# Chunked attention and a top-1 mixture of experts: the opening expert chosen a batch earlier, and the outputs' transposes ahead of the next attention product

## The chip, the cores and the metric

One core of a Trainium2 chip. The metric is the time of one execution on the device, in microseconds (us); the median of several runs is given. Engines are called by their names or by the short ones of the profile: PE is TensorE's matmuls, PEld its weight loads, DVE VectorE, ACT ScalarE, POOL GpSimd, SP SyncE, which issues most transfers.

## The reference

```python
# attention: 4 batches, 8 heads, 768 tokens, head size 64; chunks of 32 queries
for c in range(nc):
    k_full = concat([mem_k, k[l_start:r_end]])    # 8 memory keys, 16 left, 32 own, 8 right
    scores = scale * q_c @ k_full.T
    a = exp(scores - max); a /= a.sum() + 1e-9
    out[chunk] = a @ v_full
x = out.transpose(0, 2, 1, 3).reshape(3072, 512)
# mixture of experts: 8 experts, 512 -> 1024 -> 512, one expert for each token
logits = x @ w_gate + modality_bias[modality_id]
e_idx = argmax(logits); gate = softmax(logits)[e_idx]
for e in range(8):
    out[mask] = gate[mask] * (relu(x[mask] @ w1[e]) @ w2[e])
```

All is float32. The expert of a token is known only when all its heads are done.

## The kernel before, in words

**Attention.** 16 units of two heads, each in two halves (hf) of 384 tokens, make 32 iterations i. In iteration i TensorE is given, in this order: `scores` of i (L351), `exps_t` of i-1 (L369, transposes of the scores less their maximum; ScalarE then writes their exponentials, PT), the transposes of the next unit's keys (`trans_k`, hf=0, copied by ScalarE into kbd, four copies) or queries (`trans_q`, hf=1, two copies to qT), `attend` of i-1 (L381, which reads PT and v, tile vw), and `trans_x` of i-2 (L404), which transposes the normalized outputs xb for the router; ScalarE copies them to xT. VectorE takes maximum and difference (mx, sb) of i, and den, reciprocal and xb of i-1 (`normalize`). Only in iterations 29 and 30 does trans_x stand ahead of attend. The rows of xb are written to DRAM, xd, once for each unit (POOL issues).

**Routing.** When a batch's four units are done, `route(b)` is appended to a list, and `pump` issues its pieces in between: logits (L541), transposes of them, argmax on VectorE, ranks of the tokens by matmul (L581 to L586), one-hot tiles l and a (L654, L656, two of six pairs on POOL, four on VectorE), and matmuls (L664) that put token numbers into `table`. The last batches are issued faster than others (KB = 3 for batch 2).

**Start of the experts.** Slots of 256 tokens with one expert each follow. Weights are split into a high and a low part, three products for each of the two layers, with ScalarE casting and VectorE or POOL subtracting. Which expert slot 0 takes is chosen in route(2), from the counts of three batches; its place (regs0) is read by SP, which then issues the eight w1 transfers of 256 KB (`load_w(0, 0)`), and by POOL, which gathers the rows (`gather(0)`, indirect transfers). At the end of iteration 29 a loop `while routing` issues all that is left of routing ahead of these two; route(3) follows among the first mm1, the matmuls of the first layer.

**Order.** TensorE, SP and POOL run in the order in which the code is written. ScalarE and VectorE do so until iteration 26 (MAN), and from there to the second slot a scheduler orders them.

Of the kernel before, what the change touches and what calls it, by code (L numbers as in the profile page):

```python
# [9 lines left out]
F32 = mybir.dt.float32  # L10
F32R = mybir.dt.float32r
BF16 = mybir.dt.bfloat16
I32 = mybir.dt.int32
# [7 lines left out]
P = 128  # L21
# [8 lines left out]
EMPTY = 4096.0  # L30
MAGIC = 12582912.0
NTAIL = 8
NEXTRA = 7
HEAD = 3
LAST = 3
ROW_R1 = HEAD + NTAIL + 1
# [5 lines left out]
NACT = 2  # L42
CPOOL = (10, 12, 13, 14, 15)
MAN = 26
KB = 3
NSPIN = 11
NR = 32
# [6 lines left out]
def tile_chunk_attention_top1_moe(  # L54
# [129 lines left out]
    listed, turn0, ends, tail_no, at_r1, at_x = (rows[:, i:i + 1] for i in range(6))  # L184
    quarter, edge = [const.tile([P, 1], F32, name=f"quarter{i}") for i in range(2)]
    noth = const.tile([64, E], F32, name="noth")
    col0 = const.tile([64, E], F32, name="col0")
    nsl = const.tile([1, 2], I32, name="nsl")
    regs0 = const.tile([1, 2], I32, name="regs0")
# [224 lines left out]
    def pump(k, pe=False):  # L414
        k *= KB if routing and routing[0][2] == B - 2 else 1
        while k > 0 and routing:
            g, wait, b, since = routing[0]
            if wait:
                if not pe or now[0] < since + (wait == "late" or b < B - 2) + (wait == "late" and b < B - 2):
                    return  # L420
                pe = False
            r = next(g, None)
            if r is None:
                routing.pop(0)
                return
            routing[0] = (g, r if r != "v" else "", b, now[0])
            k -= r == "v"
# [14 lines left out]
    def plan_early():  # L442
        vec = nc.vector
        full = rounded("full", 1.0 / 256, 127.0 / 256 - 0.498)
        free, score, top, one, three, row = (
            plan_new("free"), plan_new("score"), plan_new("top", 1), plan_new("one"), plan_new("three", 3, E), plan_new("row", 3))
        vec.tensor_sub(free, full, ohg[0:64])
        vec.scalar_tensor_tensor(score, free, 0.0, prio, op0=ALU.is_gt, op1=ALU.mult)
        vec.reduce_max(top, score, axis=AX.X)
        vec.tensor_scalar(one, score, top, None, op0=ALU.is_equal)  # L450
        vec.tensor_tensor(three, base, one.unsqueeze(1).to_broadcast([64, 3, E]), op=ALU.mult)
        vec.reduce_sum(row, three, axis=AX.X)
        vec.tensor_copy(regs1, row)

    def plan_rest():
# [1 line left out]
        vec = nc.vector  # L457
        full, free, used = plan["full"], plan["free"], plan["one"]
        vec.tensor_sub(free, free, used)
        vec.tensor_add(used, used, ohg[0:64])  # L460
        tail = rounded("tail", 1.0 / 256, 0.498)
        vec.tensor_sub(tail, tail, full)
        small, score, top, first = plan_new("small"), plan["score"], plan["top"], plan_new("first")
# [72 lines left out]
    def route(b):  # L536
# [77 lines left out]
        yield "v"  # L614
        nc.vector.tensor_add(ac, ac, hi)
        yield "v"
        if b == B - 2:

            cm = sm.tile([P, 1], F32, name="cm")
            cb = sm.tile([P, E], F32, name="cb")  # L620
            nc.vector.tensor_copy(cb, rk[:, NT, :])
            yield "v"
            nc.vector.reduce_max(cm, cb, axis=AX.X)
            yield "v"
            nc.vector.tensor_scalar(cb, cb, cm, None, op0=ALU.is_equal)
            yield "v"
            nc.vector.tensor_mul(cb, cb, rev[:, 0])
            yield "v"
            nc.vector.reduce_max(cm, cb, axis=AX.X)
            yield "v"  # L630
            nc.vector.tensor_scalar(regs0[:, 0:1], cm[0:1], -1.0, float(E), op0=ALU.mult, op1=ALU.add)
            yield "v"
            nc.vector.tensor_scalar(regs0[:, 1:2], cm[0:1], -float(HI), float(E * HI), op0=ALU.mult, op1=ALU.add)
            yield "v"
# [29 lines left out]
            nc.tensor.matmul(tb[:, 0:192], l1, a1, start=(t == 0), stop=(t == NT - 1))  # L664
        nc.vector.tensor_sub(table if b < B - 1 else tab_i[:, 0:192], table, tb[:, 0:192])
        yield "v"
        if b == B - 2:
            nc.vector.tensor_scalar(ohg, rev[:, 0], cm, None, op0=ALU.is_equal)
            yield "v"
            nc.vector.tensor_scalar(noth, rev[0:64, 0], cm[0:64], None, op0=ALU.not_equal)  # L670
            yield "v"
            nc.vector.scalar_tensor_tensor(prio, ohg[0:64], 16.0, rev[0:64, 0], op0=ALU.mult, op1=ALU.add)
            yield "v"
            nc.vector.tensor_copy(base[:, 0], iota[0:64, 0:E])
            yield "v"
            nc.vector.tensor_copy(base[:, 1], noth)
            yield "v"
            nc.vector.scalar_tensor_tensor(base[:, 2], ohg[0:64], 2.0, col0, op0=ALU.mult, op1=ALU.add)
            yield "v"
        if b < B - 1:  # L680
            ts = sm.tile([P, E], F32, name="ts")
# [48 lines left out]
    def keep(opening):  # L730
        if not opening:
            nc.gpsimd.tensor_copy(ix_out, ix_now)  # L732
            nc.gpsimd.tensor_copy(gate_out, gate_now)  # L733
        nc.gpsimd.tensor_copy(ix_now, ix)  # L734
        for t in range(2):
            nc.gpsimd.tensor_copy(gate_now[:, t:t + 1], xg[t][:, DM:DM + 1])  # L736

    def gather(row):
        src, reg = (table, regs0[0:1, 1:2]) if row == 0 else (tab_i, (regs1 if row < 2 else regs)[row:row + 1, 2:3])
        rows = N - S if row == 0 else N  # L740
        col = nc.values_load(reg, engines=[mybir.EngineType.Pool], min_val=0, max_val=E * HI - 2,
                             skip_runtime_bounds_check_because="clamped to the table on chip")
        nc.gpsimd.tensor_copy(ix, src[:, ds(col, 2)])
        nc.gpsimd.tensor_scalar(gx, ix, float(rows - 1), None, op0=ALU.min)  # L744
        for t in range(2):
            nc.gpsimd.indirect_dma_start(  # L746
                out=xg[t], out_offset=None, in_=xd[0:rows],
                in_offset=bass.IndirectOffsetOnAxis(ap=gx[:, t:t + 1], axis=0))

    def gather_rest(i):  # L750
        row = (ROW_R1 - 1, ROW_R1)[i]
# [146 lines left out]
    for i in range(n + 2):  # L898
        live = i < n
        u, hf = units[i] if live else (NU, i % 2)  # L900
        now[0] = i
        if i == MAN:
            man.close()
        if live and i < n - 1:
            scores(u, hf)
        if 1 <= i <= n:
            exps_t(*units[i - 1])
        if live:
            less_max(u, hf)
            pump(1)  # L910
        if u + 1 < NU and hf == 0:
            trans_k(u + 1)
            regroup_q(u + 1)
            pump(3)
            store_k(u + 1, 1, 0, nc.scalar.copy)
            store_k(u + 1, 0, 0, nc.scalar.copy)
            store_k(u + 1, 0, 1, nc.scalar.copy)
            store_k(u + 1, 1, 1, nc.scalar.copy)
            pump(3)
        elif u + 1 < NU:  # L920
            share_v(u + 1)
            if u + 2 < NU:
                mem_keys(u + 2, nc.gpsimd)
            trans_q(u + 1)
            store_q(u + 1, 0)
            store_q(u + 1, 1)
            pump(5)
        elif live:
            pump(5)
        first = i in (n - 3, n - 2)  # L930
        if first:
            trans_x(*units[i - 2])
        if i == n - 2:
            scores(*units[i + 1])
        if 1 <= i <= n:
            attend(*units[i - 1])
        if i == n:
            trans_x(*units[i - 2])
            trans(0)
            trans(1)  # L940
            conv(4)
            conv(5, nc.gpsimd)
            normalize(*units[i - 1])
            mm1(0)
        if i > n:
            mm1(1)
        if i >= 2 and not first and i != n:
            trans_x(*units[i - 2])
        if 1 <= i < n:
            normalize(*units[i - 1])  # L950
            pump(1)
        if i >= 2:
            u2, hf2 = units[i - 2]
            if hf2 == 1 and u2 % 4 == 3:
                routing.append((route(u2 // 4), True, u2 // 4, 0))
        if i == 1:
            routing.append((more_constants(), False, -1, 0))
        if i == 6:
            assert not routing
            bias_rows()  # L960
        if i < n:
            pump(1, True)
        if live and hf == 0:
            if 0 < u < NU - 3:
                load_qk(u + 3)
            if u >= 1 and u - 1 + NVW < NU:
                load_v(u - 1 + NVW)
        if (u, hf) == (NU - 2, 1):
            while routing:
                pump(99, True)  # L970
            c_ld.close()
            xp = ctx.enter_context(tc.tile_pool(name="xp", bufs=1, side="right"))
            ix = xp.tile([P, 2], I32, name="ix")
            gx = xp.tile([P, 2], I32, name="gx")
            xg = [xp.tile([P, XW], F32, name=f"xg{t}", align_bytes=256) for t in range(2)]
            xth, xtl = [xp.tile([P, 4, 256 + NR], F32R, name=f"xt{i}") for i in range(2)]
            hh, hl = [xp.tile([P, 8, 256], F32R, name=f"h{i}") for i in range(2)]
            load_w(0, 0)
            gather(0)
        elif u == NU - 1:  # L980
            conv(2 * hf)
            conv(2 * hf + 1, nc.gpsimd)
# [170 lines left out]
```

## Time and profile before

| | us |
|---|---|
| median of 3 runs | 443.09 (442.23 to 444.68) |
| profiled execution | 444.34 |
| its span | 442.5 |
| PE busy | 419.0 |
| DVE, ACT, POOL busy | 306.6, 269.4, 205.7 |

The span is the time from the first to the last instruction recorded. A busy PE includes pipelined matmuls whose ends are modelled. In a timeline a row's bracket is the idle time ahead of it and what ended it; in lists of waits the engine that waits, its line, the instruction waited for, the sum, the number and the longest are shown. The granted clock is given as a share of the full 2.4 GHz.

### The profile page before, as it was taken

What the parts mean: (1) busy time and instruction counts of PE and PEld (TensorE: products, weight loads), DVE (VectorE), ACT (ScalarE), POOL (GpSimd) and SP (SyncE); (2) the same over time, 40 slices, a digit from 0 to 9 for tenths busy, and PEclk for the clock granted to TensorE, in tenths of its full rate; (3) what the DMA queues carried; (4) which work ended last, traced back from release to release, by engine and by line L of the source; (5) the groups of instructions that cost most, each with busy time, mean ns of one, the idle gap of its engine ahead of it and who ended that gap; (6) DMA issues with size and microseconds to landing.
All of it is one profiled execution on the core that took longest, in us unless ns stands there. A gap on an engine that the chain in (4) does not pass through costs nothing. (4 is left out here: it accounts for less than half of the span.)

```text
span 442.5 us, 11878 instructions
## 1 busy us (share of the span) xinstructions
PE 419.0 (95%) x4053; PEld 355.7 (80%) x4053; DVE 306.6 (69%) x752; ACT 269.4 (61%) x537; POOL 205.7 (46%) x409
## 2 busy tenths in 40 slices
PE   7889999999986998999999999999999999999993
PEld 4667777777765886989888898989898988898982
DVE  7878597687796799657646366686868584959530
ACT  5857878778655763556456455666656665757521
POOL 7999769779677932651053305505031115220101
PEclk9989999999998999999999999999999999999998
DMA  7789878787465501277185977505596404340101
GB/s 203 206 234 252 243 189 256 210 236 210 122 179 175 193 4 52 96 208 233 53 259 164 246 206 243 180 13 170 127 240 229 139 5 147 99 143 1 48 1 47
DMA packets 78307, 69.31 MB, mean 157 GB/s; under 512 B 36763, under 2 KB 64563, under 8 KB 78228
## 3 DMA queue, kind: packets, MB, share of 16 engines
q1 hardware_dynamic: 71488, 48.84, 39.6%
q0 software_dynamic: 5888, 19.41, 14.2%
q8 instruction: 37, 0.61, 0.6%
q14 instruction: 42, 0.34, 0.3%
q10 hardware_dynamic: 852, 0.11, 0.2%
HBM read 81.25 MB, written 16.58 MB: 221 GB/s over the span
## 5 line engine op out<-in xcount | busy, mean ns | idle before, releaser
L803 PEld LDWEIGHTS tr<-xt,w 128*128 128x128 f32 x1152 | 140.9, 188 | 4.9 <-issue 2.7
L803 PE MATMUL tr<-xt,w 128*128 128x256 f32 (+1 forms) x1152 | 142.9, 284 | 1.9 <-PEq L1114 0.7
L813 PE MATMUL av<-wh,h 128*128 128x512 f32 x384 | 124.9, 397 | 0.0
L807 DVE SCALAR_TENSOR_TENSOR h<-tr,h 128x256 fp32r<-128x256 f32 x96 | 40.5, 422 | 66.1 <-ACT h L804 33.7
L813 PEld LDWEIGHTS av<-wh,h 128*128 128x128 f32 x384 | 72.1, 188 | 16.6 <-issue 0.4
L813 PE MATMUL av<-wl,h 128*128 128x512 f32 x192 | 75.5, 393 | 0.0
L804 ACT ACTIVATE h<-tr 128x256 fp32r<-128x256 f32 x96 | 36.7, 384 | 54.1 <-PE tr L803 42.4
L728 DVE TENSOR_TENSOR wl<-raw,wh 128x512 fp32r<-128x512 f32 x91 | 63.0, 693 | 7.2 <-ACT wh L726 0.4
L838 POOL DMA_INDIRECT out_dram<-o,ix x24 | 24.6, 1027 | 92.6 <-ACT o L834 89.5
L728 DVE TENSOR_TENSOR w<-raw,w 128x512 fp32r<-128x512 f32 x93 | 60.2, 686 | 5.3 <-ACT w L726 2.8
L301 POOL COPY vw<-vw 24x384 f32<-24x384 f32 (+1 forms) x128 | 60.1, 506 | 3.0 <-DMA vw<-in_v_dram 1.2
L726 ACT CAST wh<-raw 128x512 fp32r<-128x512 f32 x96 | 59.0, 615 | 0.4 <-DMA raw<-in_moe_w_dram 0.4
L726 ACT CAST w<-raw 128x512 fp32r<-128x512 f32 x96 | 52.9, 622 | 0.0
L343 ACT COPY kbd<-tr 64x672 f32<-64x672 f32 x62 | 48.3, 779 | 5.3 <-PE tr L337 4.2
L813 PEld LDWEIGHTS av<-wl,h 128*128 128x128 f32 x192 | 36.1, 188 | 7.7
L834 ACT ACTIVATE o<-av,gate 128x512 f32<-128x512 f32 x24 | 16.2, 688 | 39.1 <-PE av L813 30.6
L381 PE MATMUL av<-vw,PT 128*32 128x130 f32 x768 | 29.8, 286 | 7.5 <-ACT PT L371 6.2
L746 POOL DMA_INDIRECT xg<-xd,gx x24 | 27.1, 1127 | 16.9 <-POOL gx L744 5.7
L381 PEld LDWEIGHTS av<-vw,PT 128*32 128x32 f32 x768 | 20.4, 112 | 11.9 <-ACT PT L371 9.9
L351 PE MATMUL sc<-kbd,qT 128*32 128x128 f32 x768 | 28.2, 281 | 1.3 <-DVE kbd L343 1.3
L371 ACT ACTIVATE PT<-tr 128x384 f32<-128x384 f32 x32 | 15.8, 493 | 20.1 <-PE tr L369 16.8
L359 DVE TENSOR_REDUCE mx<-sc 128x6 f32<-128x384 f32 x32 | 18.4, 574 | 9.7 <-PE sc L351 9.5
(250 smaller groups left out, 518.4 us busy)
## 6 DMA issues: line engine op xcount, KB each, us to landing
raw<-in_moe_w_dram SPq DMA_DIRECT2D x192, 256.0 KB
k<-in_k_dram SPq DMA_DIRECT2D x16, 384.0 KB
q<-in_q_dram SPq DMA_DIRECT2D x16, 384.0 KB
xd<-xb POOLq DMA_DIRECT2D x16, 384.0 KB
vw<-in_v_dram SPq DMA_DIRECT2D x32, 184.0 KB
xs<-xg SPq DMA_DIRECT2D x14, 256.0 KB
xq<-xs SPq DMA_DIRECT2D x28, 128.0 KB
vw<-in_mem_v_dram SPq DMA_DIRECT2D x32, 48.0 KB
```

The source lines that it names most:

```text
L301: nc.gpsimd.tensor_copy(vw[r0:r0 + 24, c + 1:c + 1 + w, d], vw[r0 + 32:r0 + 56, c:c + w, d])
L343: copy(dst.rearrange("p c (i j) -> p c i j", j=2)[:, :, :, j], win)
L351: nc.tensor.matmul(sc[32 * j:32 * j + 32, t * P:(t + 1) * P], qT[:, 32 * c:32 * c + 32], kbd[:, c].rearrange("p h m -> p (h m)"), start=Tr ...
L381: nc.tensor.matmul(avb[32 * j:32 * j + 32, t * W:(t + 1) * W], PT[:, t * P + 32 * j:t * P + 32 * j + 32], vw[:, c, 0:W], start=True, stop= ...
L726: nc.scalar.copy(wh[i], raw[i])
L728: (eng or nc.vector).tensor_sub(wl[i][:, s], raw[i][:, s], wh[i][:, s].bitcast(F32))
L746: nc.gpsimd.indirect_dma_start(out=xg[t], out_offset=None, in_=xd[0:rows], in_offset=bass.IndirectOffsetOnAxis(ap=gx[:, t:t + 1], axis=0))
L803: nc.tensor.matmul(pw, wt[i][:, j * P:(j + 1) * P], x[:, c, 0:w], start=(n == 0), stop=(n == 11))
L804: nc.scalar.activation(hh[:, f], ph, AF.Relu)
L807: nc.vector.scalar_tensor_tensor(hl[:, f], ph, 0.0, hh[:, f].bitcast(F32), op0=ALU.max, op1=ALU.subtract)
L813: nc.tensor.matmul(pos[t], x, w[8 + f], start=(f == 0 and n == 0), stop=(f == 7 and n == 2))
L838: nc.gpsimd.indirect_dma_start(out=out, out_offset=bass.IndirectOffsetOnAxis(ap=to[:, t:t + 1], axis=0), in_=outs[t], in_offset=None, boun ...
```

## The change

The choice of slot 0's expert and its first row of the table (regs0) moves from route(2) to route(1). A flag `enough` says whether the chosen expert has 256 tokens by then; `used0` replaces the one-hot `ohg` where full slots are counted. The gather of slot 0 reads rows of the first two batches only; its row numbers are taken in route(1) by `first_rows`. load_w(0, 0) stands behind load_v(15). The loop that issued all routing at the end of iteration 29 is gone, and so is the order of routing around it. trans_x stands ahead of attend in all iterations up to 31. NEXTRA guards one more slot.

```diff
-NEXTRA = 7
+NEXTRA = 8
+FIRST = 1
+ROWS0 = (FIRST + 1) * S
...
-        vec.tensor_sub(free, full, ohg[0:64])
+        vec.tensor_sub(free, full, used0)
...
-        vec.tensor_add(used, used, ohg[0:64])
+        vec.tensor_add(used, used, used0)
...
-        if b == B - 2:
+        if b == FIRST:
...
+            yield "v"
+            nc.vector.tensor_scalar(enough, cm[0:64], 255.5, None, op0=ALU.is_gt)
...
-        if b == B - 2:
+        if b == FIRST:
+            first_rows()
...
-            nc.vector.scalar_tensor_tensor(base[:, 2], ohg[0:64], 2.0, col0, op0=ALU.mult, op1=ALU.add)
+            nc.vector.tensor_scalar(used0, ohg[0:64], enough, None, op0=ALU.mult)
+            yield "v"
+            nc.vector.scalar_tensor_tensor(base[:, 2], used0, 2.0, col0, op0=ALU.mult, op1=ALU.add)
...
-        nc.gpsimd.tensor_copy(ix_now, ix)
+        nc.gpsimd.tensor_copy(ix_now, ix0 if opening else ix)
...
+    def first_rows():
+        col = nc.values_load(regs0[0:1, 1:2], engines=[mybir.EngineType.Pool], min_val=0, max_val=E * HI - 2,
+                             skip_runtime_bounds_check_because="clamped to the table on chip")
+        nc.gpsimd.tensor_copy(ix0, table[:, ds(col, 2)])
+        nc.gpsimd.tensor_scalar(gx0, ix0, float(ROWS0 - 1), None, op0=ALU.min)
...
     def gather(row):
+        if row == 0:
+            rows, at = ROWS0, gx0
...
-                in_offset=bass.IndirectOffsetOnAxis(ap=gx[:, t:t + 1], axis=0))
+                in_offset=bass.IndirectOffsetOnAxis(ap=at[:, t:t + 1], axis=0))
...
-        first = i in (n - 3, n - 2)
-        if first:
+        if 2 <= i < n:
             trans_x(*units[i - 2])
...
-        if i >= 2 and not first and i != n:
+        if i > n:
             trans_x(*units[i - 2])
...
+            if u == NU - 3:
+                load_w(0, 0)
         if (u, hf) == (NU - 2, 1):
-            while routing:
-                pump(99, True)
...
-            load_w(0, 0)
             gather(0)
```

TensorE's order in two iterations of the attention, before (trans_q is L315, attend L381, trans_x L404):

```order
L351 MATMUL sc<-kbd_124,qT 32x128 x12
L369 MATMUL tr<-ident,sb 128x128 x3
L315 MATMUL tr<-ident,qr 128x128 x6
L381 MATMUL av<-vw_127,PT 32x130 x12
L404 MATMUL tr<-ident,xb 128x128 x3
```

And after, where the same lines are L356, L374, L320, L386 and L409:

```order
L356 MATMUL sc<-kbd_124,qT 32x128 x12
L374 MATMUL tr<-ident,sb 128x128 x3
L320 MATMUL tr<-ident,qr 128x128 x6
L409 MATMUL tr<-ident,xb 128x128 x3
L386 MATMUL av<-vw_127,PT 32x130 x12
```

trans_x and attend have changed places; nothing else moved here.

TensorE's order in iterations 29 to 31, before. The L664 are the table matmuls of batch 2, their right-hand names the one-hot tiles:

```order
L381 MATMUL av<-vw_128,PT 32x130 x12
L664 MATMUL tr<-a_2580,l_2579 128x192
L664 MATMUL tr<-a_2588,l_2587 128x192
L664 MATMUL tr<-a_2592,l_2591 128x192
L664 MATMUL tr<-a_2596,l_2595 128x192
L664 MATMUL tr<-a_2600,l_2599 128x192
L664 MATMUL tr<-a_2625,l_2624 128x192
L351 MATMUL sc<-kbd_125,qT 32x128 x12
L369 MATMUL tr<-ident,sb 128x128 x3
L404 MATMUL tr<-ident,xb 128x128 x3
L351 MATMUL sc<-kbd_125,qT 32x128 x12
L381 MATMUL av<-vw_128,PT 32x130 x12
```

After, from the scores of iteration 30 (the table matmuls are L671):

```order
L356 MATMUL sc<-kbd_125,qT 32x128 x12
L374 MATMUL tr<-ident,sb 128x128 x3
L409 MATMUL tr<-ident,xb 128x128 x3
L356 MATMUL sc<-kbd_125,qT 32x128 x12
L386 MATMUL av<-vw_128,PT 32x130 x12
L671 MATMUL tr<-a_2677,l_2676 128x192
L671 MATMUL tr<-a_2681,l_2680 128x192
L671 MATMUL tr<-a_2685,l_2684 128x192
L671 MATMUL tr<-a_2689,l_2688 128x192
L671 MATMUL tr<-a_2693,l_2692 128x192
L671 MATMUL tr<-a_2697,l_2696 128x192
L374 MATMUL tr<-ident,sb 128x128 x3
```

The table matmuls stand one attend and two scores later.

VectorE's order at the same place, before: the one-hot pairs (L654, L656), then den to xb of iteration 28.

```order
L362 TENSOR_TENSOR sb<-sc,mx 128x384
L654 TENSOR_SCALAR l_2591<-iota,lo 128x128
L656 TENSOR_SCALAR a_2592<-iota,ac,tokm 128x192
L654 TENSOR_SCALAR l_2595<-iota,lo 128x128
L656 TENSOR_SCALAR a_2596<-iota,ac,tokm 128x192
L654 TENSOR_SCALAR l_2599<-iota,lo 128x128
L656 TENSOR_SCALAR a_2600<-iota,ac,tokm 128x192
L654 TENSOR_SCALAR l_2624<-iota,lo 128x128
L656 TENSOR_SCALAR a_2625<-iota,ac,tokm 128x192
L389 TENSOR_SCALAR den<-av 128x6
```

After (L661 and L663 are the one-hot pairs, of which the first stands here):

```order
L364 TENSOR_REDUCE mx<-sc 128x6
L367 TENSOR_TENSOR sb<-sc,mx 128x384
L364 TENSOR_REDUCE mx<-sc 128x6
L367 TENSOR_TENSOR sb<-sc,mx 128x384
L394 TENSOR_SCALAR den<-av 128x6
L396 RECIPROCAL den<-den 128x6
L401 TENSOR_TENSOR xb<-av,den 128x384
L661 TENSOR_SCALAR l_2684<-iota,lo 128x128
L663 TENSOR_SCALAR a_2685<-iota,ac,tokm 128x192
```

Both maxima and differences of iterations 30 and 31, and the outputs of 29, now stand ahead of the pairs.

## Rows read from the trace of the kernel before

**Rows 1.** The page: busy us, share of the span and instructions of each engine
```profile
PE 419.0 (95%) x4053; PEld 355.7 (80%) x4053; DVE 306.6 (69%) x752; ACT 269.4 (61%) x537; POOL 205.7 (46%) x409
```
**Rows 2.** Waits of PE, 10 to 128 us: line, releaser, sum, times, longest
```profile
PE av L381 <- ACT PT L371: 2.8, 7, 0.8
```
**Rows 3.** Timeline of PE: start, duration, instruction, idle time ahead
```profile
100.43 1.10 PE L315 MATMUL tr<-ident,qr 128*128 128x128 f32 x6
101.87 0.87 PE L381 MATMUL av<-vw,PT 128*32 128x130 f32 x24 [0.35 <-ACT PT L371]
102.68 0.55 PE L404 MATMUL tr<-ident,xb 128*128 128x128 f32 x3
103.15 0.86 PE L351 MATMUL sc<-kbd,qT 128*32 128x128 f32 x24
...
109.31 0.87 PE L381 MATMUL av<-vw,PT 128*32 128x130 f32 x24
```
**Rows 4.** Timeline of ACT, the same pair of iterations
```profile
97.69 3.23 ACT L343 COPY kbd<-tr 64x672 f32<-64x672 f32 x4
...
101.32 0.50 ACT L371 ACTIVATE PT<-tr 128x384 f32<-128x384 f32 x1
```
**Rows 5.** Timeline of DVE, the same pair of iterations
```profile
99.41 0.28 DVE L654 TENSOR_SCALAR l<-iota,lo 128x128 fp32r<-128x128 f32 x1
...
99.93 0.15 DVE L389 TENSOR_SCALAR den<-av 128x6 f32<-128x6 f32 x1
...
100.55 0.54 DVE L396 TENSOR_TENSOR xb<-av,den 128x384 f32<-128x384 f32 x1
```
**Rows 6.** Timeline of PE near 23 us
```profile
23.68 1.52 PE L381 MATMUL av<-vw,PT 128*32 128x130 f32 x22 [1.30 <-POOL vw L301]
```
**Rows 7.** Stretches: busy time by engine (x count), granted clock, DMA share, GB/s
```profile
24.00:28.00 4.00, 4.00 (x52) 2.87 (x46) 2.63 (x16) 0.48 (x1) 3.77 (x10) 0.59 0.98 280
122.00:126.00 4.00, 4.00 (x69) 3.10 (x67) 3.92 (x23) 3.90 (x7) 2.21 (x4) 1.00 0.05 16
126.00:134.00 8.00, 6.58 (x116) 4.68 (x114) 7.26 (x18) 2.50 (x7) 6.96 (x13) 1.00 1.04 286
136.00:140.00 4.00, 2.99 (x30) 2.17 (x30) 2.45 (x7) 2.59 (x6) 2.52 (x5) 0.57 0.29 77
```
**Rows 8.** Timeline of POOL: the last copies of v
```profile
127.04 3.73 POOL L301 COPY vw<-vw 24x384 f32<-24x384 f32 x8
```
**Rows 9.** Timeline of PE, 119 to 147 us
```profile
119.84 0.19 PE L581 MATMUL tr<-tot,ones_b 128*128 128x56 bf16 x1
...
120.44 0.86 PE L351 MATMUL sc<-kbd,qT 128*32 128x128 f32 x24
...
127.40 0.58 PE L664 MATMUL tr<-a,l 128*128 128x192 f32 x3
...
130.34 0.86 PE L351 MATMUL sc<-kbd,qT 128*32 128x128 f32 x24
...
131.94 0.86 PE L351 MATMUL sc<-kbd,qT 128*32 128x128 f32 x24
...
133.40 0.55 PE L369 MATMUL tr<-ident,sb 128*128 128x128 f32 x3
136.43 0.86 PE L381 MATMUL av<-vw,PT 128*32 128x130 f32 x12 [2.48 <-ACT PT L371]
...
142.76 3.38 PE L803 MATMUL tr<-xt,w 128*128 128x256 f32 x24 [0.28 <-ACT xt L761]
```
**Rows 10.** Timelines of DVE and ACT at the same place
```profile
126.64 0.42 DVE L654 TENSOR_SCALAR l<-iota,lo 128x128 fp32r<-128x128 f32 x1
...
129.44 0.57 DVE L656 TENSOR_SCALAR a<-iota,ac,tokm 128x192 fp32r<-128x192 f32 x1
...
135.78 0.16 DVE L389 TENSOR_SCALAR den<-av 128x6 f32<-128x6 f32 x1 [1.75 <-remote]
...
135.89 0.49 ACT L371 ACTIVATE PT<-tr 128x384 f32<-128x384 f32 x1 [3.24 <-remote]
```

More of the change, by code (lines that the diff above doesn't have):

```diff
@@ L186, in tile_chunk_attention_top1_moe @@
     noth = const.tile([64, E], F32, name="noth")
+    used0 = const.tile([64, E], F32, name="used0")
+    enough = const.tile([64, 1], F32, name="enough")
+    ix0, gx0 = [const.tile([P, 2], I32, name=f"{x}x0") for x in "ig"]
     col0 = const.tile([64, E], F32, name="col0")
@@ L733, in keep @@
             nc.gpsimd.tensor_copy(gate_out, gate_now)
-        nc.gpsimd.tensor_copy(ix_now, ix)
+        nc.gpsimd.tensor_copy(ix_now, ix0 if opening else ix)
         for t in range(2):
             nc.gpsimd.tensor_copy(gate_now[:, t:t + 1], xg[t][:, DM:DM + 1])
-    def gather(row):
[L739 to L744, printed above, removed]
+    def first_rows():
[3 more added lines that the diff above has]
+        nc.gpsimd.tensor_scalar(gx0, ix0, float(ROWS0 - 1), None, op0=ALU.min)
+    def gather(row):
+        if row == 0:
+            rows, at = ROWS0, gx0
+        else:
+            rows, at = N, gx
+            reg = (regs1 if row < 2 else regs)[row:row + 1, 2:3]
+            col = nc.values_load(reg, engines=[mybir.EngineType.Pool], min_val=0, max_val=E * HI - 2,
+                                 skip_runtime_bounds_check_because="clamped to the table on chip")
+            nc.gpsimd.tensor_copy(ix, tab_i[:, ds(col, 2)])
+            nc.gpsimd.tensor_scalar(gx, ix, float(rows - 1), None, op0=ALU.min)
         for t in range(2):
```

## The prediction, made before the changed kernel was run

> **What bounds the kernel now.** I read the page's line of each engine first. TensorE is busy 419.0 of the 442.5 us, VectorE 69%, ScalarE 61% [rows 1]: the span is TensorE's instruction stream, and an edit pays where that stream stands still. The profiled execution took 444.34 us, 1.84 us more than its span and 1.25 us above the median of the runs, 443.09; I form the change against the profiled execution and carry the difference over to the median.
>
> The waits of TensorE came next. Between 10 and 128 us, the attention, it waits for ScalarE's PT 2.8 us in seven places [rows 2] and once for POOL's copies of v (below); its other waits there belong to instructions that the change leaves in place or moves by one iteration, with the same producer ahead of them.
>
> The timeline shows what these waits are. In iterations with hf=1, scores, exps_t and trans_q are issued, then attend stands 0.35 us before PT is there, then trans_x follows [rows 3]. ScalarE comes late because it is in a chain: four kbd copies, 3.23 us, then xT, then PT [rows 4], which starts at 101.32 and leaves attend to follow at 101.87. In iterations that carry routing matmuls TensorE itself is late enough, and attend has no wait (109.31 follows trans_q directly, [rows 3]). So the idle time is there only behind pairs without routing work: at 32.65, 40.02, 47.38, 70.91 and 101.87, five of equal size (the last stands in [rows 3]). A pair takes 7.44 us from 101.87 to 109.31.
>
> **The transposes moved ahead of attend, iterations 2 to 28 and 31.** No instruction is added. In the five waiting iterations trans_x, 0.55 us long and spaced 0.47 from its successor [rows 3], would now stand where TensorE idles; the wait is 0.35, so at most that is filled: 5 x 0.35 = 1.75 us. ScalarE's order is unchanged, and its chain gets shorter by the trans_x that stood between attend and the next scores. In the even iterations there is no wait to fill, and I cost the swap at nothing: the pair attend and trans_x takes the same time in either order, and normalize, which starts 0.47 us later on VectorE, has cover in the next scores and exps_t (1.2 us). What could be late next is xb, which trans_x reads: the last xb ahead of 101.87 ends at 101.09 [rows 5], and trans_x would want it at 101.53, when trans_q ends; the margin is 0.44 us. Bounds of this term: nothing, if that margin is used up or DMA sets the pair; 2.4 us, if the whole 0.47 is won in the five.
>
> At 22 us attend waits 0.35 us for PT and then 1.30 us for POOL's vw copies [rows 6]. trans_x of 0.47 fits into this gap whole, and attend's end is set by POOL as before: 0.48 us more. The gap is followed by a stretch at a granted clock of 0.59 over 4 us [rows 7], most of it at the lower of the two levels, 1.2 GHz, which cost 4 x 0.41 = 1.6 us. If the shorter gap (1.65 less 0.47) no longer ends in this, 1.6 us go too; the trace of before cannot say. The gap at 101.5 of 0.35 us left the clock at 1.00, which says only that a much smaller gap does not; I take 0.3 of the 1.6.
>
> **The choice after two batches.** It puts route(1)'s counts, not route(2)'s, behind the choice. VectorE gets two small operations more (enough, used0), some 0.2 us each by its 128x6 den of 0.15 us [rows 5], on an engine that is idle 31% of the span [rows 1]; POOL gets first_rows earlier instead of in the tail. Expert 7 leads after two batches and after three with these inputs (735 against 578, 1100 against 933 tokens), and has over 255 rows at either point, so the same slots follow and the rest of the MoE's work is unchanged. The eighth extra slot is guarded and never entered: no work, some branches.
>
> The weights: eight transfers of 256 KB now stand on SP directly behind load_v(15), and no longer behind a wait for regs0 that ends near 125. In 122 to 126 the DMA engines are at 0.05, from 126 to 134 at 1.04 [rows 7], so the eight move into an empty stretch. No cast on ScalarE waits for them before, because casts are placed late. So this is worth nothing by itself in the chain of TensorE; what it can change is the crowded stretch. load_v(15) is ahead of them on the same queue, and POOL reads it at 127.04 [rows 8], so I cost the collision at nothing (if the cover goes: about 1 us of late vw, not reaching attend at 136).
>
> **The flush removed.** Here the change costs something. Before, all routing left is issued at the end of iteration 29: table matmuls of batch 2 start at 127.40 and wait for VectorE's a three times, until scores 30 at 130.34 [rows 9]; 2.94 us for 0.9 us of work (six, three of which alone took 0.58 with the last one's tail), 2.04 lost. Then TensorE waits at attend 30, from 133.95 to 136.43, for PT [rows 9], which started at 135.89 with a release that the profile calls remote, 1.9 us after its transposes ended; VectorE's den resumed 0.1 us before it in the same way [rows 10]. What delayed both is not in the profile. Then the clock is at 0.57 from 136 to 140 [rows 7]: 2.99 us of busy time at it, 2.99 x 0.43 = 1.3 us lost.
>
> After, the batch-2 table matmuls stand behind attend 29 in iteration 30, and VectorE issues l and a only behind mx, sb of 30 and 31 and xb29. I follow it from scores 28 (120.44 before, [rows 9]). Scores 31 started 11.50 us later before; without the 2.94 and with the rank matmuls that come one iteration later (0.60, 119.84 to 120.44) it is at 9.2. mx and sb of 31 end 2.1 us behind it (131.94 to 134.03, where den's wait of 1.75 begins, [rows 9, 10]): 11.3. den 0.15, a reciprocal taken as long, xb 0.54 [rows 5], with 0.1 between them: 0.95, 12.25. Four pairs of l and a: 0.5 us each alone (99.41 to 99.93, [rows 5]) or 0.85 each (126.64 to 130.01 for four, [rows 10]): 2.0 or 3.4, so 14.25 or 15.65. One table matmul, and exps_t(30) starts at 14.55 or 15.95; before it was at 12.96 (133.40). Attend 29 ends 1.6 us behind the start of scores 31, at 10.8, so TensorE has one gap of about 3.4 to 4.8 us, with short table matmuls in it, in place of 2.04 us.
>
> From exps_t(30) to the first mm1 it was 9.36 us (133.40 to 142.76, [rows 9]). Without the remote 1.9 us and the slow clock's 1.3 it is 6.16. (trans_x(29) moves ahead of attend 30 here; I cost it at nothing, since ScalarE's PT, xT and weight casts stand between it and xt, for which the first mm1 waits, and at 0.47 won at most.) So the first mm1 comes at 20.7 to 22.1, against 22.32: 1.6 to 0.2 us won, middle 0.9. The clock fell behind a gap of 2.48 us before; behind one of 3.4 or more it may well fall again, and gives back 1.3. Half of that leaves 0.25 us won here. If the remote stall comes back as well, it is +1.9.
>
> The row behind the two paces: four l-a pairs on VectorE took 0.85 each while POOL copied vw from 127.04 on [rows 8, 10], and one at 99.41, ahead of such copies, took 0.5 [rows 5]. The Trainium skill, "SBUF — State Buffer", section "SBUF: two separate sides", gives a rule for it: VectorE in a two-port mode and GpSimd share one port pair, held whole by whichever starts first. By that rule the pairs in the new place, beside POOL's transfer and gather instructions and not its copies, would depend on what those read; by the rows it is 14.25 or 15.65, and I keep both.
>
> **Sum.** 1.75 + 0.48 + 0.3 + 0.25 = 2.8 us less: profiled 444.34 to 441.5, median 443.09 to 440.3.
>
> **Rivals.**
> First, everything is won: the clock does not fall at 24 us (1.6) nor before the MoE, l and a at the quick pace (1.6): 2.23 + 1.6 + 1.6 = 5.4, or 437.7. For it: DMA is quiet when the tail runs. Against: the gap in front of exps_t(30) grows. 0.15.
> Second, the new wait eats the gain: slow pace, clock falls again: 0.2 won at the table, 1.3 lost, 2.23 won ahead: 1.1 less, 442.0. For it: [rows 7, 10]. Against: POOL's copies are over by then. 0.25.
> Third, VectorE becomes what TensorE waits for, slower: trans_x stands in front of attend and reads xb, with a margin of 0.44 us. In iterations with routing operations on VectorE before den, xb comes later, and the wait then delays attend too. From 0.44 us on each of some 12 odd iterations would lose; at 0.2 us net each 2.4 us, no fill (0), and in the tail the slow pace with the clock's 1.3: 443.09 + 2.4 + 1.3 - 0.2 = 446.6. For it: den comes at 99.93, behind l and a, where they stand ahead of it [rows 5]. Against: VectorE is idle 31% of the span. 0.13.
> Fourth, the remote stall comes back in the tail whatever loads the DMA: 440.3 + 1.9 = 442.2. 0.07.
> By a rule of the Trainium skill, "TensorE: Matmul & The Clock Gate", section "HAM oscillation — how this bites in real kernels", an idle gap throttles the engine and the work behind it pays; the row at 136 to 140 [rows 7] shows the same, and the second rival is that case.
>
> **How the numbers follow.** The forecast has 0.40. What a measurement of this kernel can tell from no change is about 0.5%, 2.2 us: faster is below 440.9, slower above 445.3. The forecast lies 0.6 below the edge, so I put 0.32 of its 0.40 on faster and 0.08 on the same; the first rival is faster (0.15); the second and fourth are the same (0.32, of which I leave 0.03 to faster); the third is slower (0.13). Faster 0.50, same 0.37, slower 0.13. The range reaches from 437.2, just past the first rival, to 444.9, short of the third.
>
> **What the profile of after would show.** The waits of TensorE for PT between 10 and 128 fall from 2.8 us to under 1, and no wait of trans_x for xb takes their place; the raw transfers begin near 118; a wait for a of 3 to 5 us before exps_t(30); at attend 30 a wait for PT of about 0.6 and not 2.48; granted clock in the ten us behind it. I am wrong if pairs of iterations still take 7.4 us with no wait left for PT, if trans_x waits for VectorE, or if the first mm1 comes over 23 us behind scores 28.

## The result, and the profile after

The changed kernel takes 445.36 us, median of 16 runs (443.7 to 449.48); beside them the kernel before, run 16 times, takes 442.0. The ratio is 1.0079, 95% interval 1.0058 to 1.01: 0.8% slower. The forecast was 440.3 and faster. The kernel before is 1.1 us quicker over 16 runs than over the three first shown.

The profiled execution after took 444.95 us with a span of 442.9. TensorE is busy less than before, 416.2 us against 419.0 [rows 1]; so it stands still more. In the first 128 us it stands less for PT, as forecast. The waits of TensorE there, after, line and releaser, sum, times, longest:

```profile
PE tr L409 <- DVE rowc L225: 1.7, 1, 1.7
PE tr L320 <- ACT kbd L348: 1.1, 5, 0.2
PE tr L409 <- DVE xb L401: 1.1, 1, 1.1
PE av L386 <- ACT PT L376: 0.7, 1, 0.7
```

2.8 us in seven places [rows 2] are now 0.7 in one; in their place trans_x (L409) waits once for xb behind routing operations, 1.1 us, and once for xb behind VectorE's constants (rowc), 1.7, where POOL's wait was [rows 6]. What was won still shows: scores 28 start at 116.91, 3.53 us earlier than at 120.44 [rows 9]. Of these 0.60 are rank matmuls that now come behind it, and 0.73 is that this execution began sooner (its first scores start at 9.16, those before at 9.89).

The timeline of TensorE from there, after:

```profile
116.91 0.86 PE L356 MATMUL sc<-kbd,qT 128*32 128x128 f32 x24
...
127.75 0.36 PE L671 MATMUL tr<-a,l 128*128 128x192 f32 x1 [0.51 <-POOL a L663]
129.32 0.47 PE L671 MATMUL tr<-a,l 128*128 128x192 f32 x2 [1.22 <-POOL a L663]
130.23 1.32 PE L671 MATMUL tr<-a,l 128*128 128x192 f32 x3 [0.43 <-DVE a L663]
131.38 0.64 PE L374 MATMUL tr<-ident,sb 128*128 128x128 f32 x3
...
138.59 3.33 PE L822 MATMUL tr<-xt,w 128*128 128x256 f32 x24 [0.67 <-ACT xt L780]
...
166.37 0.30 PE L804 MATMUL tr<-ident,xg 128*128 128x128 f32 x1 [2.17 <-DMA xg<-xd,gx]
167.84 0.98 PE L804 MATMUL tr<-ident,xg 128*128 128x128 f32 x7 [1.18 <-DMA xg<-xd,gx]
...
366.33 13.12 PE L822 MATMUL tr<-xt,w 128*128 128x256 f32 x96 [2.58 <-issue]
```

Four places are to be read here. The table matmuls of batch 2 (L671) wait, first for POOL's one-hot tiles and at the end for VectorE's; between 127.2 and 131.4 TensorE has only these six to do, about 0.9 us of work by the prediction's reckoning. The first mm1 starts 4.17 us earlier than at 142.76 [rows 9]. The transposes of slot 1's gathered rows then wait 2.17 and 1.18 us. And at 366 us, where a branch skips the guarded extra slots, TensorE stands 2.58 us and the profile names no releaser. The same places before:

```profile
169.34 0.30 PE L785 MATMUL tr<-ident,xg 128*128 128x128 f32 x1 [0.42 <-DMA xg<-xd,gx]
170.73 0.98 PE L785 MATMUL tr<-ident,xg 128*128 128x128 f32 x7 [1.10 <-DMA xg<-xd,gx]
...
367.20 11.60 PE L803 MATMUL tr<-xt,w 128*128 128x256 f32 x96 [0.55 <-PEq L1120]
```

Behind three of these the granted clock falls. Stretches of 2 us after (columns as in [rows 7]):

```profile
132.00:134.00 2.00, 2.00 (x28) 1.25 (x26) 0.01 (x1) 1.49 (x3) 0.88 (x1) 0.50 0.69 169
...
170.00:172.00 2.00, 2.00 (x9) 1.81 (x8) 1.93 (x8) 1.29 (x3) 0.00 (x0) 0.50 0.00 0
...
368.00:370.00 2.00, 2.00 (x11) 2.00 (x11) 0.83 (x2) 0.89 (x2) 0.10 (x1) 0.50 0.95 359
```

0.50 is 1.2 GHz. In the kernel before the clock stood at 1.00 from 164 to 176 and from 360 to 376.

The lead over the kernel before, between the two profiled executions, is 4.17 us at the first mm1 and 2.89 at slot 1's transposes (170.73 less 167.84). It is 0.87 behind the guard (367.20 less 366.33), and the spans end 0.4 the other way. So the gap took 2.0 us of it, and 1.27 went behind the gap, where the 96 matmuls take 13.12 us in place of 11.60.

### The profile page after: what moved, and what is told of

The parts are those of the page before. It is cut to its first block, busy times and chain, and to the rows that moved or that the text cites. A ratio compares the mean times of both kernels' runs of the same rounds, so it can differ in the third digit from the quotient of the medians.

```text
span 442.9 us, 11892 instructions
## 1 busy us (share of the span) xinstructions
PE 416.2 (94%) x4053; PEld 356.6 (80%) x4053; DVE 309.7 (70%) x754; ACT 268.9 (61%) x537; POOL 204.6 (46%) x409
## 5 line engine op out<-in xcount | busy, mean ns | idle before, releaser
L386 PE MATMUL av<-vw,PT 128*32 128x130 f32 x768 | 29.4, 287 | 1.4 <-ACT PT L376 1.4
L356 PE MATMUL sc<-kbd,qT 128*32 128x128 f32 x768 | 27.6, 277 | 1.5 <-DVE kbd L348 1.3
L386 PEld LDWEIGHTS av<-vw,PT 128*32 128x32 f32 x768 | 20.2, 113 | 7.5 <-issue 3.8
L356 PEld LDWEIGHTS sc<-kbd,qT 128*32 128x32 f32 x768 | 20.7, 111 | 5.1 <-issue 3.4
```

The source lines that it names most:

```text
L356: nc.tensor.matmul(sc[32 * j:32 * j + 32, t * P:(t + 1) * P], qT[:, 32 * c:32 * c + 32], kbd[:, c].rearrange("p h m -> p (h m)"), start=Tr ...
L386: nc.tensor.matmul(avb[32 * j:32 * j + 32, t * W:(t + 1) * W], PT[:, t * P + 32 * j:t * P + 32 * j + 32], vw[:, c, 0:W], start=True, stop= ...
```

## The experiments

Theory at the start: the guard costs 3 to 4 us, and the rest of the change a little or nothing. Rival: the gap at the guard, and the loss with it, comes from the changed opening. Ratios are to the kernel before on the same chip.

**e1_seven** and **e2_before_eight**: the number of guards alone, in the changed kernel and in the kernel before.

```diff
-NEXTRA = 8        (e1, in the changed kernel)
+NEXTRA = 7
-NEXTRA = 7        (e2, in the kernel before)
+NEXTRA = 8
```

> The changed kernel with seven guarded extra slots in place of eight; everything else as changed. Guard theory: the longer stretch that TensorE's branch skips makes its gap ahead of the last whole slots 2.58 us in place of 0.55, and the lower clock behind it costs 1.7 more; with seven, both go, and the time falls by about 3.7 us to 441.6 (ratio to before 0.997 to 1.001). Rival, that this gap comes from the transfers or the order of the changed opening: the gap stays at 2.6 and the time at 445 (ratio 1.008).

> The kernel before with eight guarded extra slots in place of seven, nothing else. Guard theory: gap of about 2.6 us at the branch and the lower clock behind it, 442.0 to 445.7 (ratio 1.008). Rival, that the gap comes from the changed opening: no change, ratio 1.000.

e1: 442.33 us, 1.0011 (0.9997 to 1.0024). e2: 444.44 us, 1.0055 (1.003 to 1.008). The timeline of TensorE at the guard, e1:

```profile
365.88 11.81 PE L822 MATMUL tr<-xt,w 128*128 128x256 f32 x96 [0.55 <-PEq L1137]
```

and e2:

```profile
365.78 13.13 PE L803 MATMUL tr<-xt,w 128*128 128x256 f32 x96 [2.90 <-issue]
```

The gap comes and goes with the constant, in either kernel. It is 2.4 us of the time by the ratio of e2 (2.6 by its median and the 441.87 beside it), and 3.0 by the changed kernel and e1 (445.36 less 442.33): less than the 3.7 I expected from the profile. The rival is refuted for the gap. But e1 is still no faster than the kernel before.

**e3_before_trans** and **e4_choice_alone**: the two halves of the rest, each with seven guards.

```diff
-        first = i in (n - 3, n - 2)        (e3, in the kernel before)
-        if first:
+        if 2 <= i < n:
             trans_x(*units[i - 2])
...
-        if i >= 2 and not first and i != n:
+        if i > n:
             trans_x(*units[i - 2])
```

e4 is the changed kernel with these lines as they were before, and NEXTRA = 7.

> The kernel before with the outputs' transposes ahead of the attention product in all iterations, the choice still after three batches, seven guards. If the transposes pay what they fill (2.2 us): the first matmul of the first layer comes 2 us earlier, the ratio is 0.995. If what they win is waited for again at the gather of the second slot, or TensorE now waits for the normalized outputs: ratio 0.999 to 1.001, and the gap ahead of slot 1's transposes grows by as much.

> The changed kernel with seven guards and with the transposes where they were before: the choice after two batches, its weights and the removed flush alone. If the early choice wins 2 us ahead of the first layer (4.2 in all less 2.2 of the transposes): first matmul of the first layer near 140.8 in place of 142.8, and the ratio between 0.996 and 1.000, lower the less of it is lost at the gather of the second slot. If the choice costs: ratio over 1.002.

e3: 440.96 us, 0.9994 (0.9972 to 1.0017); its first mm1 starts at 137.29. e4: 443.28 us, 1.0036 (1.002 to 1.0053): the early choice by itself costs. The transposes come out at 0.9 us less by medians and 0.3 by the ratio, and the interval holds no change as well. By medians -0.9, +1.4 and the guard's 2.6 to 3.0 add up to 3.1 to 3.5, with 3.4 measured.

The tail of e4 spends eight microseconds at the lower clock:

```profile
134.00:142.00 8.00, 6.52 (x62) 4.58 (x63) 3.51 (x10) 3.93 (x8) 3.43 (x7) 0.50 0.32 92
```

**e5_flush, e6_late_w, e7_fill**: three parts of the early choice, each in e1.

```diff
         if (u, hf) == (NU - 2, 1):                     (e5)
+            now[0] = i + 1
+            while routing:
+                pump(99, True)
...
-            if u == NU - 3:                            (e6)
-                load_w(0, 0)
...
+            load_w(0, 0)
             gather(0)
...
+        for _ in range(26 if b == B - 2 else 0):       (e7)
+            nc.tensor.matmul(tb[:, 256:512], ones_b, ones_b.unsqueeze(1).to_broadcast([P, 2, P]), start=True, stop=True)
         for t, (l1, a1) in enumerate(hot):
```

> The changed kernel with seven guards, and the loop that issues all routing of batch 2 at the end of iteration 29 put back: table matmuls after attend 28, one-hot pairs on VectorE ahead of the outputs of iteration 28. Choice and weights stay early. If what the early choice costs is the wait for the one-hot tiles in iteration 30 and the low clock behind it: first matmul of the first layer at 137 to 139 us in place of 141.6, and 1 to 2 us less than with seven guards alone (ratio to before 0.996 to 0.999). Rival, that the cost is in the early weights or behind the first layer, at the gather: ratio 1.000 to 1.002 as with seven guards alone.

> The changed kernel with seven guards, and slot 0's first-layer weights loaded where they were before, ahead of the gather at iteration 29; the choice stays early. If the early weights are worth nothing to TensorE: ratio as with seven guards alone, 1.001. If their place behind load_v(15) delays v and the last attends, this is faster, 0.998. If they spare the crowded stretch at 126 to 134 us, this is slower by 0.5 to 2 us, 1.002 to 1.005.

> The changed kernel with seven guards and 26 extra bf16 matmuls of 256 columns, of no use to the result, ahead of the table matmuls in iteration 30, about 2.8 us, put where TensorE otherwise stands and waits for the one-hot tiles. If the clock's fall there is what costs: the granted clock stays at 1.00 from 130 to 140 us, and the time is 1 to 2 us less than with seven guards alone (0.997 to 0.999). Rival, that the wait itself is the cost and the clock little: no gain, 1.001 to 1.003.

e5: 444.89 us, 1.008 (1.0051 to 1.0108), the opposite of what I expected. The table matmuls stand where they did before, but routing of batch 2 comes an iteration later in the changed kernel, and POOL's tiles are not ready. TensorE in e5:

```profile
128.97 0.53 PE L671 MATMUL tr<-a,l 128*128 128x192 f32 x1 [3.90 <-POOL a L663]
130.55 1.38 PE L671 MATMUL tr<-a,l 128*128 128x192 f32 x5 [1.05 <-POOL a L663]
```

POOL works its queue in order: in the changed kernel the eight copies of v stand ahead of its l and a, which end at 129.27. In the kernel before, POOL made them from 123.79 to 126.97, ahead of the copies at 127.04 [rows 8]. POOL after:

```profile
122.32 3.66 POOL L306 COPY vw<-vw 24x384 f32<-24x384 f32 x8
126.09 0.61 POOL L661 TENSOR_SCALAR l<-iota,lo 128x128 fp32r<-128x128 f32 x1
126.69 1.00 POOL L663 TENSOR_SCALAR a<-iota,ac,tokm 128x192 fp32r<-128x192 f32 x1
...
128.27 1.00 POOL L663 TENSOR_SCALAR a<-iota,ac,tokm 128x192 fp32r<-128x192 f32 x1
```

So the loop that the change removed cannot be put back by itself: with routing an iteration later, the new place of the table matmuls is the better of the two (e5 beside e1).

e6: 441.65 us, 0.9998 (0.9983 to 1.0012), where e1 has 1.0011. The early weights bring nothing that these runs can tell.

e7: 441.2 us, 0.9991 (0.9973 to 1.0009). Stretches of e7 beside e1, over the tail; e7:

```profile
130.00:142.00 12.00, 10.12 (x114) 8.28 (x112) 9.03 (x22) 7.16 (x15) 9.20 (x14) 1.00 0.54 163
```

and e1:

```profile
130.00:140.00 10.00, 7.15 (x67) 4.90 (x68) 5.77 (x18) 2.89 (x6) 6.21 (x10) 0.73 0.32 95
```

With work of no use in the wait, the clock stays at 2.4 GHz. The first mm1 comes 20.52 us behind scores 28, in e1 22.54; the two waits at slot 1's transposes then take back 1.1 of these 2.0 (2.14 and 1.14 in e7, 1.09 and 1.08 in e1). The time falls by 1.1 us by medians and 0.9 by the ratios, and the intervals overlap: about what the trace leaves, but not clear of noise by the times alone.

**e8_before_nine, e9_eight_fill, e10_before_six**: why eight guards cost.

```diff
-NEXTRA = 7
+NEXTRA = 9      (e8, in the kernel before)   NEXTRA = 8 in e7's code (e9)   NEXTRA = 6 (e10, in the kernel before)
```

> The kernel before with nine guarded extra slots. If the gap at the branch grows with the stretch skipped: over 2.9 us at the guard, about 5. If it depends on where the code behind it comes to lie: any of 0.5 to 3, not in step with the number.

> As e7_fill (26 matmuls of no use to the result ahead of the table matmuls), with eight guards: the changed kernel plus the fill. The 52 instructions more on TensorE shift all code behind them. If the gap at the guard comes from where the code behind the branch lies in memory: it is 0.55 us here, or another value than 2.6, and the time is that of e7_fill, ratio 0.999. If it comes from eight slots being skipped, wherever they lie: 2.6 us and the lower clock again, ratio 1.005 to 1.007.

> The kernel before with six guarded extra slots. If eight was a bad place for the code: a gap of about 0.55 us, as with seven and nine, or a long one at another bad place. If the gap grew with the stretch skipped, it would be under 0.55.

The timeline of TensorE at the guard, e8:

```profile
366.74 3.44 PE L803 MATMUL tr<-xt,w 128*128 128x256 f32 x27 [0.55 <-PEq L1120]
```

e9:

```profile
366.23 11.64 PE L824 MATMUL tr<-xt,w 128*128 128x256 f32 x96 [0.55 <-DVEq L1139]
```

and e10:

```profile
363.67 11.63 PE L803 MATMUL tr<-xt,w 128*128 128x256 f32 x96 [0.55 <-PEq L1120]
```

With six, seven and nine slots skipped the gap is 0.55 us, with eight 2.6 and 2.9; and with eight slots and 52 instructions more on TensorE ahead of them it is 0.55 again (e9: 441.48 us, 0.9997, 0.9977 to 1.0018, beside e7's 0.9991). e8 and e10 ran once each, 443.92 and 440.85 us, which says nothing of a difference of this size. So the gap does not grow with the number of slots. What e9 changes at this branch is where the code lies. That this is the cause is inferred: no run moves the code and nothing else. The Trainium skill, "Runtime: NRT & Kernel Launch", section "Instruction fetch mechanics", says that a taken branch to a target outside of the instructions already held forces a fetch of the target's page first. That agrees with a gap that depends on position; which part of the fetch is long at eight and short at six, seven and nine, these runs do not show. One rival stands untested. POOL issues a gather just ahead of the branch and SP the next weights behind it. In the long gap after, such transfers already run before TensorE starts at 366.33 (DMA share 1.05 over 364.83 to 365.33); in the short one of e9 they do not (0.00 over 365.73 to 366.23, where TensorE starts). Whether they lengthen the gap, or only fall into one that is long anyway, no run separates.

**e11_two_fills, e12_trans_fill**: a fill of the same kind ahead of slot 1's transposes, in e7 (18 matmuls) and in e3 (10).

```diff
-    def trans(half):
-        t = bank().rearrange("p (c n) -> p c n", c=2)
+    def trans(half, fill=0):
+        t = bank()
+        for _ in range(fill):
+            nc.tensor.matmul(t[:, 0:256], ones_b, ones_b.unsqueeze(1).to_broadcast([P, 2, P]), start=True, stop=True)
+        t = t.rearrange("p (c n) -> p c n", c=2)
...
-            trans(0)
+            trans(0, 18)      (e11; 10 in e12)
```

> e7_fill with 18 more bf16 matmuls of 256 columns, of no use to the result, ahead of slot 1's transposes, about 1.9 us in the place where TensorE waits 2.1 us for the gathered rows. If the lower clock behind that wait costs: granted clock 1.00 from 164 to 176 in place of 0.86, and 1 to 1.7 us less than e7_fill, ratio 0.995 to 0.997. If not: ratio 0.999.

> The kernel before with the transposes moved (e3_before_trans) and 10 matmuls of the same kind ahead of slot 1's transposes, 1.1 us in a wait of 1.05. If the clock behind that wait costs: 1.00 in place of 0.86 from 164 to 176, and 1 to 1.7 us less than e3_before_trans, ratio 0.996. If not: 0.999.

e11: 440.6 us, 0.9974 (0.9954 to 0.9994). e12: 440.46 us, 0.9974 (0.9951 to 0.9998). The stretch that was at 0.86 in e7 and in e3 is at 1.00; e11:

```profile
164.00:176.00 12.00, 10.43 (x77) 8.94 (x76) 11.48 (x54) 5.10 (x11) 3.10 (x9) 1.00 0.16 46
```

The fill brings 0.5 to 0.6 us by medians in either, less than the 1 to 1.7 I expected and within overlapping intervals. Both end 0.3% below the kernel before, with intervals that just exclude no change; e12 does so without the early choice.

## Why the prediction was wrong

The step that failed is the sentence on the guards: "The eighth extra slot is guarded and never entered: no work, some branches." It was costed at nothing, without a bound, although the trace of before has TensorE standing 0.55 us at that very branch. It measured 2.4 us in e2 and 3.0 in the changed kernel, and without it (e1) the time is 442.33, within the range and near the second rival's 442.0. That nearness is no success of the rival's sum: it was formed from 443.09, and the kernel before took 441.87 beside e1.

The guard is half of the miss. The change was to win 2.8 us, and e1 loses 0.5: the other 3.3 us are terms of the sum, above all the 0.25 won at the table, and the 0.48 at 22 us.

Point by point:

- The transposes. TensorE's waits for PT fell as forecast. From scores 5 to scores 24, the stretch of the five waits, the kernel before takes 73.06 us (30.09 to 103.15) and the changed one 70.91 (28.68 to 99.59): 2.15 less, where 1.75 was forecast and 2.4 was the bound. The 0.48 at 22 us did not come: trans_x, now ahead of attend, waits there for xb itself, and from scores 3 to scores 4 it is 6.55 us after and 6.53 before. And from scores 24 to scores 28 it is 17.32 and 17.29, although 0.60 of rank matmuls have left this stretch: 0.6 are lost where trans_x waits 1.1 us for xb. That 2.2 are left at scores 28 (3.53 less 0.60 and 0.73), as in the sum, is in part luck: the slow clock near 24 us, which belongs to neither kernel (below), cost this execution less (scores 4 to scores 5 take 3.62 us, before 4.12). By time only 0.9 us by medians is left (e3), with an interval that holds zero.
- The table's wait. The path was followed rightly: exps_t(30) starts 14.47 us behind scores 28, with 14.55 forecast at the quick pace; from there to the first mm1 it is 7.21 us, with 6.16 forecast and 1.3 for the slow clock; and the first mm1 comes 21.68 behind scores 28 (116.91 to 138.59). I did not look at POOL's queue, and the first two waits are for POOL's tiles; but VectorE's last pair, which ends at 131.14, sets the end. What failed is the 22.32 us that this was set against, one execution with the remote stall and a slow clock. Three others have the same code up to there. e2 and e10 took 19.55 and 19.47 (119.14 to 138.69, 119.55 to 139.02), at a clock of 1.00 and with a PT wait of 0.64. e8 took 21.05 (120.95 to 142.00), with the same PT wait and no stall, but a clock of 0.86 over 130 to 142. The tail of e2:

```profile
119.14 0.86 PE L351 MATMUL sc<-kbd,qT 128*32 128x128 f32 x24
...
133.28 0.87 PE L381 MATMUL av<-vw,PT 128*32 128x130 f32 x24 [0.64 <-ACT PT L371]
...
138.69 3.36 PE L803 MATMUL tr<-xt,w 128*128 128x256 f32 x24 [0.28 <-ACT xt L761]
```

  I had 0.2 to 1.6 us won here and 0.25 in the sum; against e2 and e10 2.1 and 2.2 are lost. 0.60 of this are the rank matmuls, which the sum charged here without the 0.60 that scores 28 come earlier for it. I took a stall that one execution showed, and that nothing in the profile named, for part of the kernel. So at the first mm1 nothing is won: from the first scores to there it is 129.43 us after, 129.46 in e2 and 129.23 in e10.
- The clock. It fell behind the gap in the table's wait in the profiles of the changed kernel, e1, e4 and e6, and did not where the gap was filled (e7, e9, e11). It can fall in the tail of the kernel before as well: it did in e8, and not in e2 and e10. Half of 1.3 us was too little by e7, which puts it near 1 us of the time (not clear of noise). The fall near 24 us comes and goes between executions of either kernel (0.79 over 22 to 30 us in before and after, 1.00 in e2, e7 and e10), and is no part of the change.
- "The rest of the MoE's work is unchanged": the work is, its waits are not. Slot 1's rows hang on the last batch's routing and not on slot 0, so when slot 0 starts earlier, TensorE waits for them: 2.17 us in place of 0.42, and the clock falls. Of the lead of 4.17 us over the execution first read 1.28 went here. Against e2 and e10 there was no lead: from the first mm1 to the first of these transposes it is 27.78 us after, 27.08 and 27.02 there, so some 0.7 was lost. Part of it is VectorE's planning of slot 1, which now runs beside POOL's subtractions and is slower (below).
- The third rival, trans_x waiting for xb, was seen, as the prediction's sign of being wrong: once 1.1 us and once 1.7. By the stretches above it took the 0.48 and some 0.6, not the 3.4. The weights: moved into the empty stretch, nothing gained (e6), as forecast.

What stays open: why the branch stalls in two of the kernels and not in the others; what the remote stall was; and whether the transposes alone are worth something, for which e3's interval is too wide.

## What to carry to other kernels

A constant that only adds code that never runs can cost more than the edit it comes with: look at every gap at a branch, and time such an edit alone. A stall in one profile that no engine or transfer explains is a property of that execution until a second one shows it. Work that is moved forward is paid for by what it meets next: the next slot's inputs and TensorE's clock, which fell behind several of the waits here and stayed up where the wait was filled.

## What the runs showed of the hardware that was not expected

The gap of TensorE at one taken branch was 0.55 us in twelve of the kernels and 2.58 and 2.90 in two, and did not follow the length of the code skipped. (In e12 a second stop of 0.70 us, again with no releaser named, comes 1.9 us behind it.)

The length of a wait does not tell by itself whether the clock falls: at slot 1's transposes it was 0.86 over 164 to 176 behind waits of 1.05 and 1.12 us in e3, and 1.00 behind 1.09 and 1.08 in e1.

And six of VectorE's smallest operations took three times as long beside POOL's as without: two of them, of slot 1's planning after, while POOL subtracts,

```profile
151.79 0.50 DVE L443 TENSOR_SCALAR full<-counts 64x8 f32<-64x8 f32 x1
...
153.89 0.49 DVE L452 TENSOR_TENSOR free<-full,used 64x8 f32<-64x8 f32 x1
```

```profile
145.89 8.47 POOL L738 TENSOR_TENSOR wl<-raw,wh 128x128 fp32r<-128x128 f32 x20
```

and the same before, behind POOL's run:

```profile
156.69 0.18 DVE L438 TENSOR_SCALAR full<-counts 64x8 f32<-64x8 f32 x1
...
157.30 0.15 DVE L447 TENSOR_TENSOR free<-full,ohg 64x8 f32<-64x8 f32 x1
```

From the first of the six to the operation behind them it is 2.62 us after (151.79 to 154.41) and 0.80 before (156.69 to 157.49): 1.8 us on the path to slot 1's rows. The six start every 0.42 us, the pace of POOL's 20 subtractions in 8.47 us. The Trainium skill, "SBUF — State Buffer", section "SBUF: two separate sides", has VectorE, in some of its operations, and GpSimd share one port pair, held by one at a time; the rows agree as far as the pace goes, and do not show the port. Not every pair of operations does it. Three of VectorE's right ahead of the six, beside the same subtractions, took 0.15 to 0.20 us (151.45 to 151.87), and at 99.41 us in the kernel before l and a took 0.5 us [rows 5] while POOL made its own (99.35, 1.12 us).
